# Routing attention into a cosine router: the opening of the first head pair, rearranged

## The chip, the cores and the metric

The kernel runs on one core of a Trainium2 chip. The metric is device time in microseconds of one execution, and a comparison is made on medians of several executions. The engines are named as in the profile: PE is TensorE's matmuls, PEld its weight loads, DVE is VectorE, ACT is ScalarE, POOL is GpSimd, SP is SyncE, which here issues most loads.

## The reference, cut to what matters

```python
# attention: q, k, v are (4, 8, 768, 64), centroids (8, 16, 64), all f32
q_assign = argmax(einsum('bhsd,hcd->bhsc', q / |q|, c / |c|))    # 16 clusters per head
k_assign = argmax(einsum('bhsd,hcd->bhsc', k / |k|, c / |c|))
mask = q_assign[..., :, None] == k_assign[..., None, :]
attn = softmax(where(mask, q @ k.T / 8, -1e9))
out = attn @ v                                   # -> x of shape (3072, 512)
# router: one of 8 experts per row by cosine logits, then its gated MLP
e = argmax((x / |x|) @ (emb / |emb|).T / tau)
y = gate * (relu(x @ w1[e]) @ w2[e])             # w1 (8, 512, 1024), w2 (8, 1024, 512)
```

## The kernel before, in words

The attention is done for 16 head pairs in turn: 4 batches by 4 pairs of heads, two heads on the 128 partitions. A head pair is cut into 12 units: two halves of 384 queries, six blocks of 128 keys in each. A unit is scores, then exp, then attend. `scores(i)` (L484) adds two products in one pair of PSUM banks: keys with queries (`kT`, `qT`, f32), and the mask as a product of one-hot cluster codes (`hot`, bf16), which adds a large negative number wherever the clusters differ. `expo(i)` (L495, ScalarE) makes `prob`, one of five buffers used in turn. `attend(i)` (L506) multiplies `prob` with `v` into `o_ps`, and VectorE adds the exponentials up in `acc` (L515, L525). The tile tag `s_ps` has two buffers of two banks, `o_ps` has one, and `misc()` hands out two single banks, misc0 and misc1, in turn.

Before a head pair's first unit its data must be prepared by the pieces of `prep_pieces`: the turn of q and k so that the head dimension lies on partitions (`turn0`, `turn1`), the products with the normalized centroids `cnB` (`products`, L396, whose result is turned to `asn` at L405), the choice of a cluster (`choose`: `amax`, `sel`, `pm` on VectorE, then the codes `cd` on ScalarE, L419 and L422), and the turn of the codes into the table `hot`. For head pairs 1 to 15 this runs beside earlier units, with VectorE turning blocks (L386) and a transposing DMA making `hot` (L427). For head pair 0 nothing runs beside it: TensorE does the turns (`turn`, L369, with copies at L375 and L377; `turn_numbers`, L437, with copies at L444 and L445), and all is in `begin()`.

`begin()` is written out in order, and every engine takes its instructions in that order (the whole attention stands under a manual schedule). It issues the first loads: the centroids on ACT's queue, then q, k and v of pair 0 and q and k of pair 1 on SP's. `constants()` fills constants and starts `keep_up`, which is idle matmuls on constants (L228) into the bank pair `idle_ps`, which has the tag `o_ps`. Then come the norms of the centroids, the turns in the order q half 0, k half 0, q half 1, k half 1, the products, the key-query part of units 0 and 1 (`scores(m, (1,))`), the choice, six idle matmuls, the table, the mask part of units 0 and 1 and their exps. The main loop then goes on, two units at a time: scores and exps of units i+2 and i+3, pieces of the next head pairs (`between`), attends of units i and i+1. After the attention come the router and the experts' MLPs, which the change does not touch.

Of the kernel before, what the change touches and what calls it, by code (L numbers as in the profile page):

```python
# [9 lines left out]
F32 = mybir.dt.float32  # L10
# [8 lines left out]
P = 128  # L19

SQ = 32
# [18 lines left out]
def kernel(  # L40
# [136 lines left out]
    def misc():  # L177
        return bank("misc", psM)
# [5 lines left out]
    def load(n, names):  # L184
        b, hp = pairs[n]
        t = ld.setdefault(n, {})
        for nm in names:
            x = t[nm] = ldp.tile([P, NJ, 2, D], F32, tag=nm + "32", name=nm + "32")
            for h in range(2):
                rows = {"q": q, "k": k, "v": v}[nm][b, 2 * hp + h]  # L190
                if nm == "v":

                    r = rows.rearrange("(i j a t) d -> a i t j d", i=2, a=2, t=SQ)
                    for g in range(P // SQ):
                        nc.sync.dma_start(
                            out=x[SQ * g : SQ * g + SQ, :, h], in_=r[g // 2, g % 2]
                        )
                    continue
                if n == 0:
                    nc.sync.dma_start(  # L200
                        out=x[:, :, h], in_=rows.rearrange("(j p) d -> p j d", p=P)
                    )
                    continue


                for w in range(D // SQ):
                    p0 = D * h + SQ * w
                    nc.sync.dma_start(
                        out=x[p0 : p0 + SQ].rearrange("p j h (o i) -> p (j h o) i", i=SQ),
                        in_=rows.rearrange("(s t) d -> t s d", t=SQ)[:, :, SQ * w : SQ * w + SQ],  # L210
                    )
# [10 lines left out]
    en_r = smp.tile([E, 1], F32, name="en_r", bufs=1)  # L222
    idle_ps = psO.tile([P, 2, 512], F32, tag="o_ps", name="idle_ps")

    def keep_up(n):

        for _ in range(n):
            nc.tensor.matmul(  # L228
                idle_ps[:, 0].rearrange("p (g x) -> p g x", x=P),
                lhsT=onesb,  # L230
                rhs=bc(onesb, [P, 4, P], 1),
                start=True,
                stop=True,
            )
# [12 lines left out]

    def constants():
        nc.vector.memset(onesb, 1.0)
        keep_up(9)  # L250
        nc.vector.memset(epsc, EPS)
        make_identity(nc, ident)
        nc.gpsimd.iota(io_i, pattern=[[1, P]], base=0, channel_multiplier=0)

        nc.gpsimd.iota(
            tok_i.rearrange("p (b j) -> p b j", j=NJ),
            pattern=[[S, B], [P, NJ]],
            base=0,
            channel_multiplier=1,
        )  # L260
        for i, (p0, w) in enumerate(((0, -BIG), (D, -2.0))):
            nc.gpsimd.memset(wcd[p0 : p0 + D], w)
        make_identity(nc, identb)
        nc.gpsimd.memset(cd, 0.0)
        for i, (p0, c) in enumerate(((0, -BIG), (D, -1.0))):
            nc.gpsimd.memset(cd[p0 : p0 + D, :, :, 2 - 2 * i : 3 - 2 * i], c)
        make_upper_triangular(nc, sltb, val=1.0, diag=False)
        for prob in probs:
            nc.gpsimd.memset(prob[:, :, HS:HE], EPS)
        nc.gpsimd.memset(gate_p, 0.0)  # L270
        nc.vector.memset(cnB, 0.0)
        nc.vector.memset(ones, 1.0)
        nc.vector.memset(embT, 0.0)
        nc.vector.memset(cumx[:, 0], 0.0)
        nc.vector.tensor_copy(io_b, io_i)
        nc.vector.tensor_copy(io_f, io_i[:, 0:SQ])
        nc.vector.tensor_scalar(prefc, io_b[:, 0:C], -1.0, float(C), ALU.mult, ALU.add)
        nc.vector.tensor_scalar(prefe, io_b[:, 0:E], -1.0, float(E), ALU.mult, ALU.add)
# [44 lines left out]
    def begin():  # L323

        nc.scalar.dma_start(out=c_sb, in_=centroids.rearrange("h c d -> (h c) d"))
        load(0, "q")
        load(0, "k")
        load(0, "v")
        load(1, "qk")
        constants()  # L330

        nc.scalar.activation(en_r, epsc[0:E], ACTF.Sqrt)
        nc.scalar.dma_start(out=emb, in_=moe_expert_emb)
        nc.scalar.dma_start(out=tau, in_=moe_tau.to_broadcast([E, 1]))
        norm_rows(cn_r, c_sb, P)
        unit_centroids()
        keep_up(2)
        piece(0, "turn0")
        piece(0, "turn1")
        norm_rows(en_r, emb, E)  # L340

        nc.scalar.activation(cn_r, epsc, ACTF.Exp)
        piece(0, "products")
        for m in range(2):
            scores(m, (1,))
        piece(0, "choose")
        keep_up(6)
        piece(0, "turn_numbers")
        for m in range(2):
            scores(m, (0,))  # L350
            expo(m)
        token_numbers()
        unit_experts()

    def prep_pieces(n):
# [8 lines left out]
        def turn(nm, half):  # L364
            if half == 0:
                t[nm + "T"] = trp.tile([P, S], F32, tag=nm + "T", name=nm + "T")
            bk = misc()
            for j in range(NJ // 2):
                nc.tensor.transpose(  # L369
                    bk[:, P * j : P * j + P],  # L370
                    t[nm][:, NJ // 2 * half + j].rearrange("p h d -> p (h d)"),
                    ident,
                )
            if nm == "q":
                nc.scalar.copy(t["qT"][:, HS * half : HS * half + HS], bk[:, 0:HS])  # L375
            else:
                nc.vector.tensor_copy(  # L377
                    in_halves(t["kT"])[:, half], bk[:, 0:HS].rearrange("p (s t) -> p s t", t=SQ)
                )

# [26 lines left out]
        def choose():  # L407

            shp = [P, S // SQ, C]
            asn = t["asn"].rearrange("p (g c) -> p g c", c=C)  # L410
            amax = smp.tile(shp[0:2], F32, tag="amax", name="amax")
            sel = smp.tile(shp, BF16, tag="sel", name="sel", bufs=1)
            pm = smp.tile(shp[0:2], BF16, tag="pm", name="pm")
            nc.vector.tensor_reduce(amax, asn, axis=AXX, op=ALU.max)
            nc.vector.tensor_tensor(sel, asn, bc(amax, shp, 2), ALU.is_equal)
            nc.vector.tensor_tensor(sel, sel, bc(prefc, shp, 1), ALU.mult)
            nc.vector.tensor_reduce(pm, sel, axis=AXX, op=ALU.max)
            pm = pm.rearrange("p (s h) -> p s h", h=2)
            nc.scalar.activation(cd[..., 1], pm, ACTF.Copy, scale=wcd)  # L419
            for i, p0 in enumerate((0, D)):  # L420
                g = slice(p0, p0 + D)
                nc.scalar.activation(  # L422
                    cd[g, :, :, 2 * i], pm[g], ACTF.Square, scale=(BIG**0.5, 1.0)[i]
                )
            t["H"] = trp.tile([P, S // (2 * SQ), P], BF16, tag="hot", name="hot")
            if n > 0:
                nc.sync.dma_start_transpose(  # L427
                    out=t["H"], in_=cd.rearrange("p s h c -> p (s h c)")
                )

        def turn_numbers():

            U = S // (4 * SQ)
            for half in range(2):
                bk = misc().bitcast(BF16)
                for u in range(U):
                    nc.tensor.transpose(  # L437
                        bk[:, P * u : P * u + P],
                        cd[:, U * half + u].rearrange("p h c -> p (h c)"),
                        identb,  # L440
                    )
                bk = bk[:, 0 : P * U].rearrange("r (s x) -> r s x", x=P)
                ss = slice(U * half, U * half + U)
                nc.scalar.copy(t["H"][:, ss, D:], bk[:, :, D:])  # L444
                nc.vector.tensor_copy(t["H"][:, ss, 0:D], bk[:, :, 0:D])  # L445

        return {
            "turn0": lambda: turn_blocks("q") if n else (turn("q", 0), turn("k", 0)),
            "turn1": lambda: turn_blocks("k") if n else (turn("q", 1), turn("k", 1)),
            "products": products,  # L450
            "choose": choose,
            "turn_numbers": turn_numbers,
# [39 lines left out]
    def expo(i):  # L492
        d = un[i]
        d["prob"] = probs[i % len(probs)]
        nc.scalar.activation(d["prob"][:, :, 0:HS], d["s_ps"][:, :, 0:HS], ACTF.Exp, scale=scale)  # L495
# [830 lines left out]
    def piece(n, name, *args):  # L1326
        if n < NP:
            if n not in prepare:
                prepare[n] = prep_pieces(n)
            prepare[n][name](*args)  # L1330

    def between(n, it):
        b, nb = divmod(n, NHP)
# [68 lines left out]
    with tc.manual_schedule(engines=by_hand):  # L1402
        begin()
        for i in range(0, len(units), 2):
# [5 lines left out]
                load(n + 1, "v")  # L1410
            if it >= 4 and n + 3 < NP:
                load(n + 3, "qk"[it - 4])
            for m in range(i + 2, min(i + 4, len(units))):
                scores(m)
                expo(m)
            between(n, it)
# [223 lines left out]
```

## Time and profile before

| | us |
|---|---|
| median of 3 timed executions | 705.94 (705.63 to 707.8) |
| profiled execution, its own time | 709.17 |
| its span | 707.4 |
| TensorE busy in the span | 692.3 |
| VectorE, ScalarE, GpSimd busy | 382.0, 264.5, 263.0 |
| packets of k's second head all landed | 6.87 after the span's start |
| first masked score begins | 15.96 |
| first attend begins | 19.99 |

The times of the view in the lower rows are counted from the start of the span. The profiled execution is one execution and is somewhat longer than the timed ones, so a sum over its rows is compared with 709.17 first.

### The profile page before, as it was taken

The numbers are of one execution on the slowest core, as the hardware profiler recorded it, in microseconds if no ns is written. First come the engines' busy times: TensorE is split into PE (matmuls) and PEld (weight loads), VectorE is DVE, ScalarE is ACT, GpSimd is POOL, SyncE is SP. The second block draws the span as 40 slices with busy tenths as digits, with TensorE's granted clock in tenths as the row PEclk, the third lists the DMA queues.
The fourth block names the chain that finished last, engine by engine and source line by source line (L and its number), as shares of the span: only waits on it lengthen the run. The fifth ranks groups of instructions, "written<-read, shape, count | busy, mean of one in ns | idle before, by whom it ended". The sixth has DMA issues, their size and how long they took to land.

```text
span 707.4 us, 16123 instructions
## 1 busy us (share of the span) xinstructions
PE 692.3 (98%) x6518; PEld 455.4 (64%) x6518; DVE 382.0 (54%) x665; ACT 264.5 (37%) x446; POOL 263.0 (37%) x402
## 2 busy tenths in 40 slices
PE   7999999999999999999999999999999999999997
PEld 3444444444444444454966668897979797979694
DVE  4688888998889999998583121240220303030310
ACT  4566655577566655676315110101010111111111
POOL 2122221322224221454224446656264454635403
PEclk9999999999999999999999999999999999999999
DMA  9546656776657787779799977268758486869360
GB/s 148 84 65 105 105 99 100 139 158 114 100 92 158 125 147 157 158 188 331 172 317 347 333 281 271 71 241 288 258 211 305 183 312 220 313 228 341 123 247 31
DMA packets 244123, 135.54 MB, mean 192 GB/s; under 512 B 207808, under 2 KB 207810, under 8 KB 244044
## 3 DMA queue, kind: packets, MB, share of 16 engines
q1 hardware_dynamic: 237852, 121.28, 63.8%
q0 software_dynamic: 6016, 13.12, 5.3%
q8 instruction: 54, 0.88, 0.5%
q14 instruction: 25, 0.20, 0.1%
q10 hardware_dynamic: 176, 0.05, 0.0%
HBM read 115.92 MB, written 13.12 MB: 182 GB/s over the span
## 4 chain that ended last, share of the span: by engine, by line
PE 80%; DVE 6%; issue 5%; DMA 5%; another core or an unknown queue 1%; ACT 1%; POOL 1%; SPq 1%; POOLq 0%; DVEq 0%; ACTq 0%
PE s_ps L484 19%; PE o_ps L506 15%; PE h_ps L1261 10%; PE y_ps L1277 9%; PE h_ps L1176 9%; PE y_ps L1213 5%; PE misc L1213 5%; PE x_ps L1176 3%; DMA out_dram<-ys,spidx 3%; DVE acc L525 2%; PE misc L553 2%; PE misc L396 2%; DMA x_rows<-xb 1%; PE misc L632 1%
## 5 line engine op out<-in xcount | busy, mean ns | idle before, releaser
L495 ACT ACTIVATE prob<-s_ps 128x768 f32<-128x768 f32 x192 | 153.5, 811 | 97.1 <-PE s_ps L484 83.4
L484 PE MATMUL s_ps<-qT,kT 64*64 64x384 f32 x1536 | 156.8, 484 | 0.0
L506 PE MATMUL o_ps<-prob,v 64*64 64x385 f32 x1536 | 142.0, 486 | 0.0
L525 DVE TENSOR_TENSOR acc<-acc,prob 128x768 f32<-128x768 f32 x128 | 125.7, 982 | 8.8 <-ACT cd L422 0.5
L506 PEld LDWEIGHTS o_ps<-prob,v 64*64 64x64 f32 x1536 | 54.7, 133 | 70.2 <-issue 58.4
L1222 DVE STREAM_TRANSPOSE ys<-y_ps 128x256 f32<-128x256 f32 (+4 forms) x16 | 6.6, 414 | 155.4 <-PE y_ps L1213 138.7
L1261 PE MATMUL h_ps<-xTm,w1s 128*128 128x128 f32 x768 | 88.6, 275 | 1.4 <-issue 1.4
L1261 PEld LDWEIGHTS h_ps<-xTm,w1s 128*128 128x128 f32 x768 | 87.6, 192 | 3.0 <-issue 2.6
L1277 PE MATMUL y_ps<-w2s,hT 128*128 128x512 f32 x192 | 85.3, 594 | 1.7 <-ACT hT L1268 1.0
L539 POOL TENSOR_TENSOR o_sum<-o_sb 128x385 f32<-128x385 f32 x30 | 31.4, 1048 | 148.1 <-ACT o_sb L530 148.1
L1052 POOL DMA_INDIRECT out_dram<-ys,spidx x56 | 56.9, 1017 | 74.1 <-DVE ys L1236 59.4
L484 PEld LDWEIGHTS s_ps<-qT,kT 64*64 64x64 f32 x1536 | 56.4, 134 | 38.5 <-issue 35.3
L1268 ACT ACTIVATE hT<-h_ps 128x512 f32<-128x512 f32 x24 | 14.3, 596 | 162.9 <-PE h_ps L1261 119.1
L1176 PE MATMUL h_ps<-xTs,w1s 128*128 128x272 f32 (+7 forms) x384 | 72.9, 346 | 1.1 <-ACTq L1537 1.1
L1176 PEld LDWEIGHTS h_ps<-xTs,w1s 128*128 128x128 f32 x384 | 66.6, 190 | 8.0 <-issue 2.4
L484 PE MATMUL s_ps<-hot 64*64 64x384 bf16 x768 | 65.5, 329 | 2.4 <-ACT prob L495 1.3
L574 POOL COPY inv<-inv 32x12 f32<-32x12 f32 x120 | 42.9, 358 | 55.2 <-DVE inv L571 50.8
L1277 PEld LDWEIGHTS y_ps<-w2s,hT 128*128 128x128 f32 x192 | 35.3, 190 | 42.9 <-issue 40.2
L1041 POOL DMA_INDIRECT xs<-x_rows,gpidx x56 | 56.4, 1007 | 17.1 <-issue 16.5
L484 PEld LDWEIGHTS <-hot 64*64 64x64 bf16 x768 | 23.7, 107 | 40.3 <-issue 39.1
L1213 PE MATMUL y_ps<-hTs,w2o 128*128 128x272 f32 (+7 forms) x256 | 48.0, 346 | 0.0
L1213 PE MATMUL misc<-hTs,w2o 128*128 128x272 f32 (+7 forms) x256 | 48.0, 346 | 0.0
(264 smaller groups left out, 680.0 us busy)
## 6 DMA issues: line engine op xcount, KB each, us to landing
w1s<-in_moe_w_dram SPq DMA_DIRECT2D x18, 2048.0 KB
w2s<-in_moe_w_dram SPq DMA_DIRECT2D x18, 2048.0 KB
v<-in_v_dram SPq DMA_DIRECT2D x128, 48.0 KB
q<-in_q_dram SPq DMA_DIRECT2D x60, 96.0 KB
k<-in_k_dram SPq DMA_DIRECT2D x60, 96.0 KB
x_rows<-xb SPq DMA_DIRECT2D x60, 96.0 KB
xr<-x_rows SPq DMA_DIRECT2D x9, 512.0 KB
w1s<-in_moe_w_dram SPq DMA_DIRECT2D x4, 1024.0 KB
```

The costliest lines, as they stand in the source:

```text
L484: nc.tensor.matmul(s_ps[D * half : D * half + D, h, 0:HS], lhsT=l[rows, half], rhs=r[rows], start=part == (1 if len(parts) < 2 else 0), st ...
L495: nc.scalar.activation(d["prob"][:, :, 0:HS], d["s_ps"][:, :, 0:HS], ACTF.Exp, scale=scale)
L506: nc.tensor.matmul(g["o_ps"][D * h : D * h + D, half, 0:HE], lhsT=ld[n]["v"][keys, j, h], rhs=d["prob"][keys, h, 0:HE], start=(j == 0), st ...
L525: nc.vector.tensor_tensor(g["acc"], g["acc"], d["prob"][:, :, 0:HS], ALU.add)
L539: add(t["o_sum"][:, hq], t["o_sb"][:, 0], t["o_sb"][:, 1], ALU.add)
L574: nc.gpsimd.tensor_copy(inv2[M * to : M * to + M, :, i % 2], inv[M * i : M * i + M])
L1041: nc.gpsimd.indirect_dma_start(out=to, out_offset=None, in_=of, in_offset=bass.IndirectOffsetOnAxis(ap=at, axis=0), bounds_check=n - 1, oo ...
L1052: inst = nc.gpsimd.indirect_dma_start(out=to, out_offset=bass.IndirectOffsetOnAxis(ap=at, axis=0), in_=of, in_offset=None, bounds_check=n - 1,
L1176: nc.tensor.matmul(bk, lhsT=w1s[it.slot][:, c, P * f : P * f + P], rhs=d["xT"][:, c, 0:C], start=(c == 0), stop=(c == KD - 1),)
L1213: nc.tensor.matmul(bks[g][:, 0:C], lhsT=d["w2"][:, f, P * g : P * g + P], rhs=d["hT"][:, f, 0:C], start=(f == 0), stop=(f == KF - 1),)
L1261: nc.tensor.matmul(bk[:, m : m + P], lhsT=w1s[it.slot][:, c, f0 + m : f0 + m + P], rhs=d["xT"][:, P * c : P * c + P], start=(c == 0), stop ...
L1277: nc.tensor.matmul(bk, lhsT=d["hT"][:, P * c : P * c + P], rhs=w2s[it.slot][:, c], start=(c == 0), stop=(c == KF - 1),)
```

## The change

All of it lies in the preparation of head pair 0 and in the first step of the main loop.

- `load`: k of pair 0 comes in two halves of three blocks for each head; the first halves are issued on ACT's queue, the second on SP's. q stays on SP's queue.
- `begin`: the norm of the centroids comes before the two small loads of the experts' data on ACT; the turns go q half 0, q half 1, then the centroids' own turn, then k half 0, k half 1. The idle matmuls are ten at the start (nine and two before); the six later ones go to a misc bank.
- `turn`: q's two halves go to the two banks of `idle_ps`, k's to the two misc banks. The copy of k's second half is on ScalarE.
- `choose`, pair 0: the two squares that fill the codes' outer columns go to VectorE as one multiplication each; the middle column stays on ScalarE.
- `turn_numbers`: both halves of the codes are turned first. The table is then copied in five pieces, those needed by the first query half ahead: columns 0 to 31 of half 0 (VectorE), columns 64 to 127 of half 0 (ScalarE), columns 0 to 31 of half 1 (VectorE). The rest follows after the first masked scores have been issued.
- scores: unit 2 gets the key-query product ahead of the masks too, in the bank pair with the tag `o_ps`; the exps go in the order 0, 2, 1, and the main loop starts with unit 3 alone.

```diff
@@ -197,9 +197,13 @@
                         )
                     continue
                 if n == 0:
-                    nc.sync.dma_start(
-                        out=x[:, :, h], in_=rows.rearrange("(j p) d -> p j d", p=P)
-                    )
+
+                    for i in range(1 + (nm == "k")):
+                        js = slice(NJ // 2 * i, NJ // 2 * i + NJ // 2) if nm == "k" else slice(0, NJ)
+                        queue = nc.scalar if nm == "k" and i == 0 else nc.sync
+                        queue.dma_start(
+                            out=x[:, js, h], in_=rows.rearrange("(j p) d -> p j d", p=P)[:, js]
+                        )
                     continue
 
 
@@ -222,11 +226,11 @@
     en_r = smp.tile([E, 1], F32, name="en_r", bufs=1)
     idle_ps = psO.tile([P, 2, 512], F32, tag="o_ps", name="idle_ps")
 
-    def keep_up(n):
+    def keep_up(n, bk):
 
         for _ in range(n):
             nc.tensor.matmul(
-                idle_ps[:, 0].rearrange("p (g x) -> p g x", x=P),
+                bk.rearrange("p (g x) -> p g x", x=P),
                 lhsT=onesb,
                 rhs=bc(onesb, [P, 4, P], 1),
                 start=True,
@@ -247,7 +251,7 @@
 
     def constants():
         nc.vector.memset(onesb, 1.0)
-        keep_up(9)
+        keep_up(10, idle_ps[:, 0])
         nc.vector.memset(epsc, EPS)
         make_identity(nc, ident)
         nc.gpsimd.iota(io_i, pattern=[[1, P]], base=0, channel_multiplier=0)
@@ -330,12 +334,11 @@
         constants()
 
         nc.scalar.activation(en_r, epsc[0:E], ACTF.Sqrt)
+        norm_rows(cn_r, c_sb, P)
         nc.scalar.dma_start(out=emb, in_=moe_expert_emb)
         nc.scalar.dma_start(out=tau, in_=moe_tau.to_broadcast([E, 1]))
-        norm_rows(cn_r, c_sb, P)
+        piece(0, "turn0")
         unit_centroids()
-        keep_up(2)
-        piece(0, "turn0")
         piece(0, "turn1")
         norm_rows(en_r, emb, E)
 
@@ -343,12 +346,17 @@
         piece(0, "products")
         for m in range(2):
             scores(m, (1,))
+        un[2]["s_ps"] = psO.tile([P, 2, 512], F32, tag="o_ps", name="s_ps2")
+        scores(2, (1,))
         piece(0, "choose")
-        keep_up(6)
-        piece(0, "turn_numbers")
-        for m in range(2):
+        keep_up(6, misc())
+        rest = piece(0, "turn_numbers")
+        next(rest)
+        for m in range(3):
             scores(m, (0,))
+        for m in (0, 2, 1):
             expo(m)
+        next(rest, None)
         token_numbers()
         unit_experts()
 
@@ -364,7 +372,7 @@
         def turn(nm, half):
             if half == 0:
                 t[nm + "T"] = trp.tile([P, S], F32, tag=nm + "T", name=nm + "T")
-            bk = misc()
+            bk = misc() if nm == "k" else idle_ps[:, half]
             for j in range(NJ // 2):
                 nc.tensor.transpose(
                     bk[:, P * j : P * j + P],
@@ -374,7 +382,7 @@
             if nm == "q":
                 nc.scalar.copy(t["qT"][:, HS * half : HS * half + HS], bk[:, 0:HS])
             else:
-                nc.vector.tensor_copy(
+                (nc.scalar.copy if half else nc.vector.tensor_copy)(
                     in_halves(t["kT"])[:, half], bk[:, 0:HS].rearrange("p (s t) -> p s t", t=SQ)
                 )
 
@@ -419,6 +427,16 @@
             nc.scalar.activation(cd[..., 1], pm, ACTF.Copy, scale=wcd)
             for i, p0 in enumerate((0, D)):
                 g = slice(p0, p0 + D)
+                if n == 0:
+                    nc.vector.scalar_tensor_tensor(
+                        out=cd[g, :, :, 2 * i],
+                        in0=pm[g],
+                        scalar=(BIG, 1.0)[i],
+                        in1=pm[g],
+                        op0=ALU.mult,
+                        op1=ALU.mult,
+                    )
+                    continue
                 nc.scalar.activation(
                     cd[g, :, :, 2 * i], pm[g], ACTF.Square, scale=(BIG**0.5, 1.0)[i]
                 )
@@ -431,6 +449,7 @@
         def turn_numbers():
 
             U = S // (4 * SQ)
+            bks = []
             for half in range(2):
                 bk = misc().bitcast(BF16)
                 for u in range(U):
@@ -439,14 +458,18 @@
                         cd[:, U * half + u].rearrange("p h c -> p (h c)"),
                         identb,
                     )
-                bk = bk[:, 0 : P * U].rearrange("r (s x) -> r s x", x=P)
-                ss = slice(U * half, U * half + U)
-                nc.scalar.copy(t["H"][:, ss, D:], bk[:, :, D:])
-                nc.vector.tensor_copy(t["H"][:, ss, 0:D], bk[:, :, 0:D])
+                bks.append(bk[:, 0 : P * U].rearrange("r (s x) -> r s x", x=P))
+            H = [t["H"][:, U * half : U * half + U] for half in range(2)]
+            nc.vector.tensor_copy(H[0][:, :, 0:SQ], bks[0][:, :, 0:SQ])
+            nc.scalar.copy(H[0][:, :, D:], bks[0][:, :, D:])
+            nc.vector.tensor_copy(H[1][:, :, 0:SQ], bks[1][:, :, 0:SQ])
+            yield
+            nc.vector.tensor_copy(H[1][:, :, SQ:], bks[1][:, :, SQ:])
+            nc.vector.tensor_copy(H[0][:, :, SQ:D], bks[0][:, :, SQ:D])
 
         return {
-            "turn0": lambda: turn_blocks("q") if n else (turn("q", 0), turn("k", 0)),
-            "turn1": lambda: turn_blocks("k") if n else (turn("q", 1), turn("k", 1)),
+            "turn0": lambda: turn_blocks("q") if n else (turn("q", 0), turn("q", 1)),
+            "turn1": lambda: turn_blocks("k") if n else (turn("k", 0), turn("k", 1)),
             "products": products,
             "choose": choose,
             "turn_numbers": turn_numbers,
@@ -1327,7 +1350,7 @@
         if n < NP:
             if n not in prepare:
                 prepare[n] = prep_pieces(n)
-            prepare[n][name](*args)
+            return prepare[n][name](*args)
 
     def between(n, it):
         b, nb = divmod(n, NHP)
@@ -1410,7 +1433,7 @@
                 load(n + 1, "v")
             if it >= 4 and n + 3 < NP:
                 load(n + 3, "qk"[it - 4])
-            for m in range(i + 2, min(i + 4, len(units))):
+            for m in range(i + 2 if i else 3, min(i + 4, len(units))):
                 scores(m)
                 expo(m)
             between(n, it)
```

## The prediction

> **What bounds the kernel now.** I read the engine totals first, then TensorE's waits by stretch, then the chain of waits of the first 25 us, then the granted clock there.
>
> The totals:
>
> ```profile
> PE 692.3 (98%) x6518; PEld 455.4 (64%) x6518; DVE 382.0 (54%) x665; ACT 264.5 (37%) x446; POOL 263.0 (37%) x402
> ```
>
> TensorE is occupied for 98% of the span. Its waits from 20 to 320 us are one row:
>
> ```profile
> PE s_ps L484 <- ACT prob L495: 0.7, 2, 0.4
> ```
>
> From 20 us on TensorE runs without gaps (from 320 us the same view lists 4.2 us in six waits). So whatever brings it earlier into that steady stretch comes off the end one for one, if the suppliers keep up. The change touches only the first 20 us. The chain of waits there (start us, length us, what):
>
> ```profile
> 2.42 4.44 DMA k<-in_k_dram
> ...
> 7.00 0.53 PE misc L369 x3
> ...
> 7.56 0.57 DVE kT L377
> ...
> 10.31 0.60 DVE asn L405
> ...
> 12.50 0.56 DVE pm L417
> ...
> 14.13 0.51 PE misc L437 x6
> ...
> 14.66 0.87 ACT hot L444 x2
> ...
> 15.55 0.37 DVE hot L445
> ```
>
> The reader is to see a serial road: k's load to 6.87, turns and products to asn (10.31), the choice on VectorE to 13.07, codes on ScalarE, turns of the codes, both table halves on two engines in turn, and only then the first masked score. TensorE in that stretch, in the timeline (start, length; idle before and releaser in brackets):
>
> ```profile
> 11.59 1.47 PE L228 MATMUL idle_ps<-onesb 128*128 128x512 bf16 x6
> 14.13 0.83 PE L437 MATMUL misc<-identb,cd 128*128 128x128 bf16 x12 [1.07 <-ACT cd L422]
> 15.96 0.85 PE L484 MATMUL s_ps<-hot 64*64 64x384 bf16 x8 [1.01 <-DVE hot L445]
> 17.41 0.54 PE L484 MATMUL s_ps<-hot 64*64 64x384 bf16 x4 [0.59 <-ACT prob L495]
> ```
>
> And the clock (stretch, us, PE, PEld, DVE, ACT, POOL, then PEclk):
>
> ```profile
> 16.00:17.00 1.00, 0.82 (x8) 0.32 (x8) 0.83 (x7) 0.46 (x1) 0.00 (x0) 0.50 1.55 142
> 17.00:18.00 1.00, 0.59 (x8) 0.53 (x11) 1.00 (x2) 1.00 (x2) 0.00 (x0) 0.50 1.52 142
> 18.00:19.00 1.00, 1.00 (x9) 0.27 (x5) 1.00 (x2) 0.06 (x1) 0.00 (x0) 0.50 1.66 163
> 19.00:20.00 1.00, 1.00 (x17) 0.66 (x13) 1.00 (x2) 0.71 (x1) 0.00 (x0) 0.80 1.03 129
> ```
>
> So from 16.0 to 19.4 TensorE runs at half clock, right when the real work begins. The first pair of attends starts at 19.99; the scores of units 4 and 5 at 21.28.
>
> **What the Trainium skill says.** "TensorE: Matmul & The Clock Gate", Part 1: the clock is set by activity in free-running windows of about 3.4 us; an idle window halves it. The trace agrees on the length (half clock for 3.41 us) and shows that a window need not be empty: 12.6 to 16.0 holds 0.5 us of idle matmuls and 0.83 us of turns, about 40% busy, and is followed by half clock, while 5.75 to 9.16, about 70% busy, is not. "Trainium Kernel Development and Optimization", Key Constraints: queues of SP and ACT share the same 16 DMA engines, a second queue saves issue time alone. Here issue is not the limit: SP issues a 768-packet load in 0.45 to 0.61 us, while the four q and k loads land at 3.92, 4.83, 5.79 and 6.87, 0.95 us apart. "PSUM — Partial Sum Buffer", on bank collisions: two engines may not access one bank and quadrant at once. The trace agrees as far as L445 waits for L444 on the same bank; the changed program's waits show the same between engines.
>
> **Part 1, loads.** Half of k (2 x 384 packets) goes to ACT's queue, behind 128 centroid packets. Landings follow about 2.85 us + packets/808 per us (896, 1664, 2432, 3200 give 3.96, 4.91, 5.86, 6.81 against the four above). With the queues served alike, ACT's k half is in at about 5.1, q's second head when 2432 packets are served: 5.86 instead of 4.83; k's second half at 6.8 as before. So q is later, k is not earlier in whole. On SP, eight v issues follow, each waiting for an earlier landing; the sixth waits for k's last (6.8), so pair 1's loads start near 8.2 instead of 7.35 and its k lands near 16.7 instead of 15.87. VectorE turns it at about 18.0: hidden. On ACT's queue the two issues come before the table load (1.28 us), so the centroid norm is 1 us later (cn at about 5.0 instead of 4.0), hidden by q's arrival. Emb and tau's issues are behind the norm; tau's waits for q's first head; both are over before the first qT copy.
>
> **Part 2, turns.** Ten idle matmuls (0.427 us each at cold clock) end issue at 5.34; TensorE then waits for q to 5.92 (5.86 before). One turn of three takes 0.49, a copy 0.48. In the changed program the second q turn still waits for the first copy (idle_ps is one tile), so: turn 5.92 to 6.41, copy to 6.91, turn 6.95 to 7.44. The centroids' turn now stands behind that: end 7.55, two cnB copies (0.46 on VectorE) to 8.04. k's second half waits for these copies (bank misc0): 8.08 to 8.57, kT copy on ScalarE to 9.09 (before: VectorE, 9.32). From that copy to asn took 0.99: asn at **10.1 instead of 10.31, gain 0.2**. Bounds: q landing at 5.3 gives 0.6; at 6.5 a loss of 0.4. I take 0.2.
>
> **Part 3, codes.** asn to the end of pm: 2.76, kept: 12.85. Then ScalarE needs one activation (wait 0.08 + 0.40) instead of three (0.08 + 0.84). The two squares go to VectorE beside it; the nearest row, L277 at 128x16, is 0.17 each, 0.35 in all, so ScalarE still ends last. Codes at 13.33, turns 0.14 later at 13.47. **Gain 0.4** (0.3 to 0.5). TensorE's cover: unit 2's product part is added before (0.73 us a unit, from 1.46 for two), so three units run 9.9 to 12.1, six idle matmuls (spacing 0.213) to 13.4: no gap is left ahead of the codes.
>
> **Part 4, table.** Twelve turns take 0.83, the first six 0.51. VectorE's copy of 192 elements is about 0.22 (0.357 for 384), ScalarE's 0.43 follows it on the same bank, VectorE's second 0.20 runs beside it. First masked score 0.51 + 0.02 + 0.22 + 0.03 + 0.43 + 0.05 = 1.26 after the turns begin; before 1.83. **Gain 0.6**: it starts at 14.73 instead of 15.96. The remaining table copies (0.5 + 0.2), four token operations and the expert ones (0.8 + 0.9) end on VectorE at about 17.1, then the turns of pair 1 (0.96 + 0.92) at 18.95, before their products at 19.9: hidden by attends 0 and 1 and scores 4 and 5.
>
> **Part 5, three units ahead and the clock.** From the masked score to the start of scores 4: before 5.32 (15.96 to 21.28). After: twelve masked matmuls at full clock, done by 15.7; exps of units 0, 2, 1 from 15.12, 0.81 each, to 15.93, 16.76, 17.57. Scores 3 wait for the first exp (its bank) to 15.97 and end at 16.8; attend 0 waits for unit 2's exp, which frees o_ps, at 16.76; attend 1 for unit 1's, 17.57, and ends at 18.26. That is 3.53, **gain 1.8**: about 1.2 of it is the half clock (replaying the old order at full clock puts scores 4 at 20.1), about 0.6 unit 2's product part, done in TensorE's old gap. The window 12.6 to 16.0 is now about 80% busy, so I expect full clock. One idle matmul fewer is worth nothing: it ran while TensorE waited for q.
>
> **Sum**: 0.2 + 0.4 + 0.6 + 1.8 = 3.0 us. The profiled execution took 709.17 (span 707.39 and 1.78 around it) and would be 706.2; the median of the runs shown is 705.94, 3.2 below it, so **702.9** there. Downstream nothing is to give it back: VectorE's queue had 3.86 us idle until 23.94, waiting for pair 1's products, which move with TensorE.
>
> **Rivals.** *Clock off in neither*: the windows run free, so timed runs of before may miss the half clock; the spread 705.63 to 707.80 allows it. Then only 3.0 - 1.2 = 1.8 comes off: 704.1. Against it: the weak stretch before, 13.06 to 17.4, holds under 1.5 us of work in 4.3, and few window phases avoid it. *A new half-clock window after*: the window 5.75 to 9.16 has about 1.1 us of gaps after the change (1.0 before). If it trips, the products, the three units and the idle matmuls end about 1.3 us late: gain 1.7, 704.2. *Slower*: q lands with k's last (6.9 instead of 5.9), adding 1.0 to the turns, TensorE then idles over half of a window, pays the 1.3, and the shifted exp waits drop a second window (3.41 x 0.5 = 1.7): -3.0 + 1.0 + 1.3 + 1.7 = +1.0, 706.9. It decides once q lands after about 6.5 and both windows fall. The packet rates speak against it. *The change doesn't do what it says*: the waits in the changed program already tie q's two turns together; if the two table engines are tied further, part 4 falls away: 703.5.
>
> **How the numbers follow.** Sum as worked out, with part 4's rival: 0.66 (its own range 702.0 to 703.8). Gain 1.2 to 2.1 through either clock rival: 0.26. Slower than before: 0.08. About 0.3%, 2.1 us, is what a measurement of this kernel can tell from no change: faster by more 0.68, within 0.28, slower by more 0.04. Range 701.6 to 705.0.
>
> **What would show it.** After: q's turns from about 5.9, asn near 10.1, codes' turns near 13.5 with hardly a gap ahead of them, the first masked score near 14.7, attends from 16.8, scores 4 at 18.3, PEclk 1.00 through 12 to 20. Wrong: PEclk 0.50 anywhere in 9 to 20, q's turns after 6.5, products of pair 1 waiting for VectorE, or new TensorE waits beyond 20 us.

## The result, and the profile after

The changed kernel took 704.38 us (median of 22 executions) against 706.45 for the kernel before (22 executions beside it): a ratio of 0.9968, 95% interval 0.9961 to 0.9976, or 2.1 us off with 1.7 to 2.8 for the interval. The forecast was 702.9 with 701.6 to 705.0 for the range: 3.0 us off the 705.94 of the three executions shown before. The sign is as forecast, the size two thirds. In the third comparison below, one of the ten executions of the changed kernel ran at a mean granted clock of 0.948 and took 724.62 us; it is left out of the numbers given there.

The profiled execution took 703.29, the lowest of the 22, with a span of 701.5. The chain of waits of the changed kernel's first 20 us (start us, length us, what):

```profile
1.26 3.98 DMA q<-in_q_dram
...
5.38 0.53 PE idle_ps L377 x3
...
5.93 0.49 ACT qT L383
...
6.46 0.55 PE idle_ps L377 x3
...
7.16 0.22 DVE cnB L307
...
7.67 0.55 PE misc L377 x3
...
11.71 1.40 PE misc L232 x6
...
13.20 0.51 PE misc L456 x6
13.71 0.03 issue
13.73 0.27 DVE hot L463
...
14.02 0.49 ACT hot L464
```

The chain now begins with q and not with k, goes over the two q turns with a ScalarE copy between them (the wait that idle_ps, one tile, imposes), the centroids' copies and k's second half. Ahead of the codes' turns it runs over the idle matmuls (to 13.11; the codes themselves are ready at 13.05), so TensorE no longer stands there; then over the first two table pieces. TensorE in the timeline (start, length; idle before and releaser in brackets):

```profile
11.64 1.47 PE L232 MATMUL misc<-onesb 128*128 128x512 bf16 x6
13.20 0.83 PE L456 MATMUL misc<-identb,cd 128*128 128x128 bf16 x12
14.55 0.68 PE L507 MATMUL s_ps<-hot 64*64 64x384 bf16 x12 [0.53 <-ACT hot L464]
15.82 0.36 PE L507 MATMUL s_ps<-hot 64*64 64x384 bf16 x4 [0.59 <-ACT prob L518]
16.63 1.80 PE L529 MATMUL o_ps<-prob,v 64*64 64x385 f32 x16
```

No idle time stands before the codes' turns (1.07 before), 0.53 us before the first masked score (1.01 before), and the first attend starts at 16.63 (19.99 before). The clock, in the same columns as before:

```profile
12.00:16.00 4.00, 2.81 (x35) 1.52 (x36) 2.90 (x14) 1.92 (x4) 0.00 (x0) 1.00 1.15 151
16.00:20.00 4.00, 4.00 (x56) 2.78 (x49) 3.15 (x5) 2.61 (x4) 0.00 (x0) 1.00 1.26 130
```

PEclk is 1.00 through 12 to 20 us. The products of pair 1 start 3.05 us earlier (before, then after, each in its own timeline):

```profile
23.02 0.52 PE L396 MATMUL misc<-qT,cnB 128*32 128x384 f32 x2
```

```profile
19.97 0.52 PE L404 MATMUL misc<-qT,cnB 128*32 128x384 f32 x2
```

TensorE's waits from 20 to 320 us stay one row, 0.3 us where before had 0.7:

```profile
PE s_ps L507 <- ACT prob L518: 0.3, 1, 0.3
```

So the lead is kept, and is 3.42 us at the last attend (331.39 against 334.81). The spans differ by 5.9 us, though; the other 2.5 us lie in the expert stage, from the last attend to the last matmul: 364.83 us against 367.34. Most of that is waits of TensorE, 4.2 us before and 2.2 after (each from 320 us on):

```profile
PE h_ps L1261 <- issue: 1.4, 2, 1.1
PE h_ps L1176 <- ACTq L1537: 1.1, 1, 1.1
PE y_ps L1277 <- ACT hT L1268: 1.0, 2, 0.6
PE y_ps L1277 <- issue: 0.7, 1, 0.7
```

```profile
PE h_ps L1199 <- ACTq L1560: 1.1, 1, 1.1
PE h_ps L1284 <- issue: 0.7, 2, 0.4
PE y_ps L1300 <- ACT hT L1291: 0.4, 1, 0.4
```

That stage is not touched, and two later profiles, one with the order of before and one of the changed kernel, took 363.12 us there alike, with 1.1 us of waits in each. So it is a difference between single executions and no gain of the change.

The 22 executions of before lie in two groups of eleven with nothing between: 705.28 to 706.01 (median 705.75) and 706.90 to 708.29 (median 707.48). The changed kernel is 1.4 us below the one and 3.1 below the other. The median of before, 706.45, lies in the gap, where no execution fell: with one more execution in either group it would have been 706.01 or 706.90, so the 2.1 us are in part the luck of an even split. The mean clocks of these 22 executions are not on record; those of later executions are. The groups are what the experiments had to explain.

### The profile page after: what moved, and what is told of

It reads as the page before. It is cut to its first block, busy times and chain, and to the rows that moved or that the text cites. A ratio compares the mean times of both kernels' runs of the same rounds, so it can differ in the third digit from the quotient of the medians.

```text
span 701.5 us, 16127 instructions
## 1 busy us (share of the span) xinstructions
PE 690.0 (98%) x6517; PEld 456.7 (65%) x6517; DVE 383.3 (55%) x668; ACT 264.0 (38%) x444; POOL 263.2 (38%) x402
## 4 chain that ended last, share of the span: by engine, by line
PE 83%; issue 5%; DMA 5%; DVE 5%; POOL 1%; ACT 1%; POOLq 0%; SPq 0%; DVEq 0%; ACTq 0%
PE s_ps L507 19%; PE o_ps L529 16%; PE h_ps L1284 10%; PE y_ps L1300 10%; PE h_ps L1199 9%; PE misc L1236 5%; PE y_ps L1236 5%; PE x_ps L1199 3%; DMA out_dram<-ys,spidx 3%; DVE acc L548 2%; PE misc L576 2%; PE misc L404 2%; PE misc L655 1%; DMA q<-in_q_dram 1%; DMA x_rows<-xb 1%
## 5 line engine op out<-in xcount | busy, mean ns | idle before, releaser
L1064 POOL DMA_INDIRECT xs<-x_rows,gpidx x56 | 56.4, 1007 | 17.1 <-issue 16.8
```

Source lines behind the costliest of these rows:

```text
L1064: nc.gpsimd.indirect_dma_start(out=to, out_offset=None, in_=of, in_offset=bass.IndirectOffsetOnAxis(ap=at, axis=0), bounds_check=n - 1, oo ...
```

## The experiments

**Theory**: an execution of before loses a 3.41 us clock window at the opening or loses none, depending on how the windows lie; the change takes about 1.5 us of serial chain out of every execution, and the lost window as well where there was one. **Rival**: the groups come from the expert stage, and the whole gain is chain. (The chain is the road of waits through the opening; "asn" with a time stands for the moment at which VectorE starts to turn the products into the tile of that name.)

The first comparison ran on a chip where all kernels were about 3 us longer and scattered more; the second and third ran on two others, where before took 704.44 and 704.09. The profiles say where the 3 us lie: TensorE waits 3.7 to 4.8 us in the expert stage in the four of the first comparison, and 1.1 us in all eight of the other two. Only numbers of one comparison are set against each other, unless said.

**The changed kernel again** (no edit), first comparison.

> The changed kernel again, on the chip of this comparison. Clock theory (before loses a half-clock window in some executions and not in others, after the change in none): before shows two groups about 1.2 to 1.8 us apart, the lower with a mean granted clock nearer 1.0; the changed kernel shows one group, about 1.3 to 1.8 us below before's lower group and 3 us below its upper one, 704.4 against a before of 705.7 or 707.5. Rival (the two groups of before come from the expert stage and have nothing to do with the opening): the changed kernel shows two groups as far apart as before's, and each lies about 2 to 3 us below its counterpart.

Measured: 707.12 against 709.68, ratio 0.9970 (0.9956 to 0.9983). Every execution comes with its mean granted clock. Of 59 executions of before 29 had 0.997 or less, with a median of 710.37, and 30 had 0.998 or more, median 708.80. One of 22 executions of the changed kernel was at 0.997 or less. A window at half clock is 3.41 x 0.5 of some 707 us, 0.0024 of the mean, so one lost window about makes the split (the mean also holds the idle end of the span, which blurs it). Against the executions of before that kept it, the changed kernel's (707.05) gain 1.75 us. That speaks for the theory; the scatter is too wide here to show the groups apart.

**Before, kept warm.** Nothing but idle matmuls is added:

```diff
-        keep_up(6)
+        keep_up(11)
         piece(0, "turn_numbers")
+        keep_up(5)
```

> The kernel before with idle matmuls alone added: eleven instead of six ahead of the codes' turns and five more behind them, so that the two 1.0 us gaps of TensorE there are filled and nothing else is touched. Clock theory: the window ahead of 16 us is busy, PEclk is 1.00 from 12 to 20 us, the first attend comes about 1.2 us earlier in an execution where before had lost the window, the upper group of before vanishes and the time is 705.6 to 705.9 (ratio 0.9985 to 0.9995). Rival (groups from the expert stage): both groups stay, the ratio is 1.000 within 0.0005, or slower by the idle matmuls, up to 0.3 us.

Measured: 709.39, ratio 0.9991 (0.9978 to 1.0004): none of 14 executions lost a window, but the median lay 0.6 above the higher-clock group of before, and 11 of the 30 executions of that group were faster than the fastest of the 14. By its time alone this speaks for the expectation's rival, that idle matmuls cost what the clock brings; with that scatter it decides little. It ran again in the third comparison, beside the changed kernel:

> The kernel before with its two gaps around the codes' turns filled with idle matmuls, once more, where the first try lay between the two groups of before. Clock theory: no execution loses a window early, and the median is that of before's higher-clock executions within 0.3 us, so 1.3 to 1.7 us below its lower-clock ones. If idle matmuls cost what the clock brings: the median lies midway or above, as in the first try.

> The changed kernel as the reference of this comparison. From the two comparisons before: executions of the kernel before whose granted clock lost no window lie 1.3 to 1.8 us above it, those that lost one 2.7 to 3.3 us; the changed kernel itself loses a window in at most 1 of 20.

Measured: 703.37, all 22 executions between 702.97 and 703.63, ratio 0.9986 (0.9979 to 0.9993). The 31 executions of before fall into three groups with gaps between: 15 from 702.87 to 703.62 (median 703.41, mean clock 0.998 to 1.0), 11 from 704.09 to 704.92 (704.76; ten of them at 0.997 or less), 5 from 705.79 to 706.60 (706.12; 0.993 or 0.994). The steps of the clock are those of one and of two lost windows. The second comparison shows the same three groups of before: 22 executions from 702.93 to 703.71, none under 0.999; 24 from 704.05 to 705.29, none above 0.998; 5 from 705.76 to 706.27, at 0.993 or 0.994. The kept-warm kernel lands on the first group, 0.04 us off, and the other groups are gone. Its two gaps are filled, in the timeline:

```profile
11.69 2.55 PE L228 MATMUL idle_ps<-onesb 128*128 128x512 bf16 x11
14.23 0.83 PE L438 MATMUL misc<-identb,cd 128*128 128x128 bf16 x12
14.90 1.24 PE L228 MATMUL idle_ps<-onesb 128*128 128x512 bf16 x5
16.07 0.52 PE L485 MATMUL s_ps<-hot 64*64 64x384 bf16 x8
```

and its clock stays up, while its chain is that of before (asn 10.41, masked score 16.07):

```profile
16.00:20.00 4.00, 3.25 (x49) 1.88 (x52) 3.83 (x12) 3.11 (x4) 0.00 (x0) 1.00 1.52 142
```

So work without any use, put into two gaps of the opening, takes 0.7 us off the median and the upper groups away. This shows that before's upper groups hang on those gaps, and the mean clocks say by what: the lost clock. The rival falls, since nothing in the expert stage was touched. Why one execution loses a window and the next does not is not shown. The changed kernel beside it took 701.93, ratio 0.9967 (0.9955 to 0.9979): 1.44 us below the kept-warm one. That is the chain's worth without the clock. In the two profiles the products of pair 1 start 1.86 apart (kept warm, then changed, each in its own timeline), and the last matmuls end at 696.33 and 694.48, 1.85 apart:

```profile
21.99 0.52 PE L397 MATMUL misc<-qT,cnB 128*32 128x384 f32 x2
```

```profile
20.13 0.52 PE L404 MATMUL misc<-qT,cnB 128*32 128x384 f32 x2
```

**The changed kernel without unit 2 ahead**, first comparison; the edit restores the two-unit loop:

```diff
-        un[2]["s_ps"] = psO.tile([P, 2, 512], F32, tag="o_ps", name="s_ps2")
-        scores(2, (1,))
...
-        for m in (0, 2, 1):
-            expo(m)
```

> The changed kernel with unit 2 not ahead of the masks: key-query products of units 0 and 1 alone go before, exps in the order 0, 1, main loop from unit 2. If the prediction's split of part 5 holds, this gives 0.6 us back at full clock, and more where the gap it leaves (about 0.7 us ahead of the codes' turns) drops the clock: 705.0, up to 706.2. If unit 2's place is worth nothing because the wait for the exps takes over: 704.4 as the changed kernel.

Measured: 708.05 against the changed kernel's 707.12, with 9 of 22 executions at a clock of 0.997 or less. (Of the changed kernel's 22 it was one.) Those that kept it took 707.49, 0.44 above their counterparts; the rest of the 0.9 is lost windows. The gap is back in the timeline, and the profiled execution lost a window, but not there: at 401 us, behind a wait of 1.9 us at the start of the expert stage (the row of its idle time ahead of the codes' turns, its wait at the start of the expert stage, and the stretch behind that with PEclk 0.50):

```profile
13.28 0.83 PE L453 MATMUL misc<-identb,cd 128*128 128x128 bf16 x12 [0.71 <-DVE cd L428]
```

```profile
PE h_ps L1281 <- issue: 1.9, 1, 1.9
```

```profile
401.00:404.00 3.00, 3.00 (x17) 3.00 (x16) 0.26 (x1) 0.20 (x1) 0.00 (x0) 0.50 1.02 403
```

So there is a second place where a window can fall, and how many of the nine fell at the opening is not known. Before's third group (2.7 us above the first in the third comparison) lost two windows by its clock. The second one could be put here, but the record doesn't support that: no profile of the third comparison has that 1.9 us wait, and the kept-warm kernel, changed at the opening alone, lost none in 22 executions. No profile of an execution of the third group was taken; where its second window fell stays open.

**Before with unit 2 ahead alone**, first comparison; the edit is the reverse of the one above, made in the kernel before, with its six idle matmuls moved to a misc bank.

> The kernel before with only the unit-2 part of the change: three units' key-query products ahead of the masks, exps 0, 2, 1, main loop from unit 3. Clock theory: the products fill 0.73 us of the 1.07 us gap, the other gap of 1.0 us stays; if that keeps the clock, 1.8 us comes off the executions that lost it and 0.6 us off the others: 705.1. If the clock still drops: 705.9 on the median. Rival in which the clock is not the point: 0.6 us off every execution, two groups kept.

Measured: 708.80 against 709.68, ratio 0.9990 (0.9975 to 1.0005), not told apart from no change by itself. Four of 14 executions lost a window (29 of 59 before); those that kept it took 708.21, 0.6 below theirs. Fewer executions lose a window with one of the two gaps filled in part (1.07 to 0.43 us), but four of 14 are too few to say how many fewer. What stays of the gaps:

```profile
14.19 0.83 PE L440 MATMUL misc<-identb,cd 128*128 128x128 bf16 x12 [0.43 <-ACT cd L425]
16.03 0.68 PE L487 MATMUL s_ps<-hot 64*64 64x384 bf16 x12 [1.00 <-DVE hot L448]
```

**Four parts undone one at a time**, second comparison (before: 704.44). Each edit puts back the old lines of one part into the changed kernel. The changed kernel itself did not run in this comparison.

Loads and turns as before (the cut shows one pair of lines; the loads, the order of the norms, the banks, the copies and the idle matmuls of these turns go back with it):

```diff
-            "turn0": ... (turn("q", 0), turn("q", 1)),
+            "turn0": ... (turn("q", 0), turn("k", 0)),
```

> The changed kernel with loads and turns as they were before: k whole on SP's queue, turns in the order q, k, q, k in the two misc banks, centroids' turn ahead of them, both k copies on VectorE. In the changed kernel's trace q's turns began at 5.38 and asn at 9.65, so this part looks worth 0.66 and not the 0.2 forecast. If that holds: asn near 10.3, codes' turns near 13.85, masked scores near 15.2, time 0.6 to 0.7 above the changed kernel. If asn only moved by the execution's luck with the loads: asn near 9.8 to 10.0 and no difference that shows.

Measured: 702.14, ratio 0.9971 (0.9961 to 0.9980). asn at 9.99, as in the expectation's second case. Its chain of waits shows what moved it: k landed at 6.55 here, at 6.87 in before's profile.

```profile
2.43 4.12 DMA k<-in_k_dram
...
6.68 0.53 PE misc L375 x3
...
9.99 0.59 DVE asn L411
```

That does not make the 0.66 between the two profiles of the result an accident, as the profile of "before with unit 2 ahead" shows, which has the same loads and turns:

```profile
2.42 4.51 DMA k<-in_k_dram
...
10.38 0.59 DVE asn L408
```

In the old order asn follows k's landing at a fixed distance, 3.44 or 3.45 in all five profiles that have it: landings at 6.55, 6.87, 6.93, 6.97 and 7.05, asn at 9.99, 10.31, 10.38, 10.41 and 10.50. The changed kernel's asn, 9.65, 9.68 and 9.82 in three profiles, hangs on q's turns and the centroids' copies instead. So the part is worth 0.2 to 0.4 where k lands as early as here (asn is 9.55 to 9.77 in the three other kernels of this comparison, which keep the changed turns), and 0.6 to 0.8 in the other four, each set against the changed kernel's profile of its own comparison.

k's halves all on SP's queue:

```diff
-                        queue = nc.scalar if nm == "k" and i == 0 else nc.sync
+                        queue = nc.sync
```

> The changed kernel with k in halves, all of them on SP's queue behind q. If the queues share the DMA engines evenly, as the prediction had it, q's second head lands here about a microsecond earlier than with two queues, q's turns begin when the idle matmuls end (5.3 to 5.4) and k's halves land later, the first at about 5.8 or after; asn within 0.2 of the changed kernel's 9.65. If the second queue adds throughput: k's last half lands later here than the 6.81 of the changed kernel, towards 7.0 or above, and asn moves to 9.8 or later.

Measured: 702.23, ratio 0.9969 (0.9959 to 0.9978). q's second head was in at 4.52 (5.24 with two queues), k's last packets at 6.75 (6.81), asn at 9.77. (The expectation's direction for q holds; k's last landing did not move, and the second of its four pieces was in at 5.44, where the first was expected at 5.8 or after.) The second queue brings nothing here: k's last packets come at the same time either way, and q's delay lies under the idle matmuls, which end at 5.52 in this profile. In the result's profile they ended at 4.97 and TensorE waited 0.41 us for q; asn, 9.65, was no later for it.

Codes on ScalarE alone:

```diff
-                if n == 0:
+                if n < 0:
                     nc.vector.scalar_tensor_tensor(
```

> The changed kernel with all three code columns on ScalarE. The forecast for the part was 0.4 at the codes' turns; in the changed kernel's trace VectorE's two multiplications took 0.54 and ended at 13.05, after ScalarE's 12.90, so the part looks worth 0.27. Expected: asn to codes' turns 3.82 instead of 3.55, time 0.3 above the changed kernel at most. Rival: the idle matmuls (to 13.1) are what the turns wait for, and nothing changes.

Measured: 701.94, ratio 0.9969 (0.9961 to 0.9977). asn to the codes' turns 3.81 instead of 3.55, as expected, and the turns wait for ScalarE:

```profile
12.39 0.40 ACT L427 ACTIVATE cd<-pm,wcd 128x24 bf16<-128x24 bf16 x1 [1.41 <-DVE pm L425]
12.61 0.61 ACT L440 ACTIVATE cd<-pm 64x24 bf16<-64x24 bf16 x2
13.36 0.83 PE L456 MATMUL misc<-identb,cd 128*128 128x128 bf16 x12 [0.35 <-ACT cd L440]
```

Table copied as before:

```diff
-            nc.vector.tensor_copy(H[0][:, :, 0:SQ], bks[0][:, :, 0:SQ])
-            nc.scalar.copy(H[0][:, :, D:], bks[0][:, :, D:])
...
+                nc.scalar.copy(H[half][:, :, D:], bks[half][:, :, D:])
+                nc.vector.tensor_copy(H[half][:, :, 0:D], bks[half][:, :, 0:D])
```

> The changed kernel with the table copied as before: each half in two pieces, ScalarE first, then VectorE, and the masked scores after all four. Forecast for the part: 0.6 (1.83 against 1.26 from the codes' turns to the masked score); in the changed kernel's trace the stretch is 1.35. If the part is what it was taken for: 1.8 here, time 0.45 above the changed kernel. If the exps on ScalarE set the pace later, part of it is lost again: 0.2.

Measured: 702.28, ratio 0.9970 (0.9961 to 0.9979). From the codes' turns to the masked score 1.84 instead of 1.35:

```profile
13.78 0.86 ACT L464 COPY hot<-misc 128x384 bf16<-128x384 bf16 x2 [0.83 <-PE misc L456]
14.29 0.74 DVE L465 COPY hot<-misc 128x384 bf16<-128x384 bf16 x2 [1.19 <-ACT hot L464]
15.09 0.68 PE L505 MATMUL s_ps<-hot 64*64 64x384 bf16 x12 [1.00 <-DVE hot L465]
```

The four medians, 701.94 to 702.28, lie 0.0 to 0.35 above the changed kernel's 701.93 of the third comparison (before's lowest group had a median of 703.44 in the second and 703.41 in the third). None of these parts shows clearly in the time by itself; their sizes are read from the stages of the profiles. A warning about the groups stands here too: three of the 20 executions with the codes on ScalarE lie at 703.17 to 703.40, about a microsecond above the rest, at a mean clock of 0.999. A step of that size is not always a lost window; what made this one is not known.

**Beyond the change**, third comparison. q's second half gets a bank pair that is free at that time:

```diff
-            bk = misc() if nm == "k" else idle_ps[:, half]
+            if nm == "k":
+                bk = misc()
+            elif half == 0:
+                bk = idle_ps[:, 0]
+            else:
+                bk = psS.tile([P, 2, 512], F32, tag="s_ps", name="turn_ps")[:, 0]
```

> The changed kernel with q's second half turned into a bank pair of its own (one of the s_ps pairs, free at that time), so that its turns need not wait for the copy of the first half (0.57 us in the changed kernel's trace). Expected, if that wait and the centroids' turn behind it hold up k's second half: k's turns follow its landing at 6.8 to 6.9 instead of starting at 7.67, asn near 8.9 instead of 9.65, the codes' turns at 12.45, unless the six idle matmuls that now end near 12.3 are what they wait for; 0.6 to 0.8 us below the changed kernel. Rival: k's load still decides and only 0.2 comes off.

Measured: 701.04 (6 executions), ratio 0.9956 (0.9941 to 0.9970), 0.9 below the changed kernel beside it. In the timeline the second q turn follows the first with no wait:

```profile
5.49 0.87 PE L382 MATMUL idle_ps<-ident,q 128*128 128x128 f32 x3
6.15 0.53 PE L382 MATMUL turn_ps<-ident,q 128*128 128x128 f32 x3
...
7.34 0.55 PE L382 MATMUL misc<-ident,k 128*128 128x128 f32 x3 [0.22 <-DVE cnB L307]
```

k's second half still waits for the centroids' copies; asn came at 9.33 (9.82 in the changed kernel's profile beside it), not at 8.9. The profiles support 0.5 us, the rest of the 0.9 is within what six executions leave open. It had the lowest median of all versions run.

The same with k all on SP's queue:

> The same with k's halves all on SP's queue, where the last landed at 6.44 instead of 6.87 and q's second head at 4.97 instead of 5.24: asn near 8.5, the codes' turns near 12.1, 0.3 us below the version with two queues, if nothing else takes over; the idle matmuls ahead of the codes would then end last. Rival: the same time as with two queues, since k's second half waits for the centroids' copies near 6.9 in both.

Measured: 701.43, ratio 0.9960 (0.9946 to 0.9974), asn 9.55. The rival holds: k's second half waits for the centroids' copies (7.52) and not for its load, which was in at 6.70 here and 6.91 with two queues. (The two landings named in the expectation, 4.97 and 6.44, were those of other pieces of k in that profile; q's second head and k's last packets were at 4.52 and 6.75, so there was little to win from the start.)

## Why the prediction came out as it did

The forecast's mechanism was right, step by step; what was off is sizes. The clock's part was counted too often, and parts 1 and 2 were taken too low. In the profiles (us gained at each step, from the start of one to the start of the next):

| step | forecast | before to changed, the result | kept-warm to changed, third comparison |
|---|---|---|---|
| parts 1 and 2, to asn | 0.2 | 0.66 | 0.59 |
| part 3, asn to the codes' turns | 0.4 | 0.27 | 0.29 |
| part 4, codes' turns to the first masked score | 0.6 | 0.48 | 0.48 |
| part 5, masked score to scores 4 | 1.8, of it 1.2 clock | 1.88 | 0.73 |
| scores 4 to pair 1's products | not priced | -0.24 | -0.23 |
| sum | 3.0, of it 1.2 clock | 3.05 | 1.86 |

The second and third columns differ by the clock: 1.15 us in part 5, forecast 1.2. That the sums fit so well is luck in part, since parts 1 and 2 gave three times their forecast and made up for the rest.

**The clock was counted in every execution.** Part 5 put 1.2 us of its 1.8 on the half clock, and the sum took the whole 3.0 off 705.94, a median that lies in the lower of before's two groups. By the reading above that group had lost no window, so there was none to win back. The prediction's own rival says 704.1 for that case; measured was 704.38. The groups were not evidence that could be had from three executions, but the spread of those three was noted. By group or by mean clock, executions without a lost window were 11 of 22, 30 of 59, 22 of 51 and 15 of 31, so about half of the term was to be counted: 3.0 less half of 1.2 is 2.4, and the measured 2.1 has 1.7 to 2.8. The argument against the rival, that few positions of the windows avoid the weak stretch, was wrong; it also read that stretch too low (13.06 to 17.4 has 1.68 us of TensorE's work in the trace, not under 1.5). In the times a lost window costs more than the 1.2: the groups lie 1.7 apart in the result, 1.4 in the second and third comparison.

**At full clock** the forecast was 1.8. The profiles of the kept-warm and the changed kernel give 1.85 at the last matmul, their medians 1.44; the lower groups of before give 1.4 in the result and 1.5 in the third comparison (1.75 in the first, with its scatter). Here the size is right to within what one profile can say, and 0.3 to 0.4 too large by the medians.

**Parts 1 and 2.** q's second head was forecast at 5.86 and landed at 5.24: the queues were not served alike, which it had assumed. k's last packets landed at 6.81, as forecast. asn was forecast at 10.1 and came at 9.65 to 9.82. What the part brings beside the forecast 0.2 is that asn no longer follows k's landing. The false wait between q's turns was there as forecast (0.57 us), and taking it out paid.

**Part 3.** The two multiplications on VectorE took 0.54 together, not 0.35, and end after ScalarE; L277 was too cheap a neighbour for them. The idle matmuls end within 0.1 us of the codes, so faster codes alone would bring little while six of them stand there.

**Part 4.** The copies took 0.26 and 0.48, forecast 0.22 and 0.43.

**Part 5.** From the masked score to scores 4, 3.44 instead of the 3.53 forecast. Attend 0 started at 16.63, forecast 16.8; scores 4 at 17.99, forecast 18.3. The stretch from 12.6 to 16.0 was 65% busy (2.21 of 3.40 us), not about 80%, and the clock held all the same.

**Downstream** was right but for one step: no new wait of TensorE after 20 us, pair 1's turns hidden, and the lead kept over 300 us of attention. Scores 4 and 5, though, take 1.98 us in the changed kernel and 1.74 before, which gives 0.24 back; the trace shows no wait there, and the cause stays open.

## What to carry to other kernels

When a kernel is bound by one engine from some point on, the opening is worth its full length, and it is read stage by stage from the chain of waits. In before's profile two gaps of 1.0 us were followed by 3.41 us at half clock, so such gaps can cost twice. Whether they do is a matter of the execution: a forecast weighs that term with the share of executions that pay it, and asks first which group the number belongs to from which it subtracts. The mean granted clock beside each time helps to tell. Filling the two gaps with idle matmuls gave a third of the change's gain (0.7 of 2.2 us in the third comparison) for two edited lines. And a part whose gain hangs on when a load lands is worth several profiles, not one.

## What the runs showed of the hardware that was not expected

- The same program loses a clock window in about half of its executions (29 of 59 by the mean clock, 29 of 51 and 16 of 31 by group) and keeps it in the others. With the gaps filled no execution of 36 (14 and 22) had a mean clock under 0.998.
- A second place, a wait of 1.9 us near 400 us, lost a window in one profile: PEclk 0.50 from 401.0 to 404.4. In the 3.41 us ahead of it TensorE was busy for 1.56 us; ahead of before's half clock, for 1.33. Neither stretch was empty.
- The same two kernels took 707.1 and 709.7 in one comparison, 701.9 and 704.1 in another, on another chip; the ratio was 0.9970 and 0.9967.
- A VectorE copy of 128x192 bf16 out of PSUM took 0.26 us, of 128x384 0.36: half the elements cost over two thirds of the time.
